# A fused gated linear attention and MLP kernel: the attention tiles of two neighbouring blocks follow each other

## The chip, the cores and the metric

The kernel runs on one core of a Trainium2 chip. Its time is device time in microseconds (us), and less is better. The engines work side by side, each through its own instructions in order: TensorE (PE in the profile; its weight loads are PEld) multiplies matrices into PSUM, VectorE (DVE), ScalarE (ACT) and GpSimd (POOL) do the rest, and SyncE (SP) issues the DMAs.

## The reference

The first part is a recurrence with a decay per key channel, for 4 batches, 8 heads, 768 steps and head size 48; the second is an MLP on its rows, 3072 x 384, with 2048 hidden units.

```
# attention: q, k, v, alpha are (4, 8, 768, 48)
for t in range(S):
    state = alpha[:, :, t, :, None] * state + einsum('bhd,bhe->bhde', k[:, :, t], v[:, :, t])
    y[:, :, t] = einsum('bhd,bhde->bhe', q[:, :, t], state)
x = y.transpose(0, 2, 1, 3).reshape(B * S, H * D)
# MLP: w_in (384, 2048), w_out (2048, 384), s and b one number each
r = maximum(x @ w_in, 0)
out = (s * r * r + b) @ w_out
```

## The kernel before

The 3072 rows are cut into 24 blocks of 128 steps, six per batch; the state is carried from block to block within a batch. For block n the work has these parts, each a small function:

- `load` (SP): four DMAs of 192 KB, for alpha, k, q and v, into rings of eight buffers. Blocks 0 to 3 are loaded two at a time (`load_pair`), and w_in and w_out in four pieces each.
- `ln` (ScalarE) takes the logarithm of alpha. `cum_pe` sums it over the steps with a triangular matrix `U_bf` on TensorE, and `cum_act` makes two exponentials of the sum. `decay`, inside `cum_act`, sends the last row through DRAM to the layout that the state needs (SP).
- `kb_mul`, `qb_mul` (VectorE) multiply k and q by these. `vcast` (GpSimd) brings v to bf16.
- `tr` (TensorE) transposes both into the bank `ct_ps`, and `qk_copy` brings them to SBUF as `qkT`.
- `amat` (TensorE, L343) makes the matrix A of one block: eight matmuls, over 48 rows each. Even heads use rows 0 to 47 of the array and write `a_ps[0]`, odd heads use rows 64 to 111 and write `a_ps[1]`. `mask` (VectorE, L352), once for each bank, multiplies A with a triangle (`mask4`) and writes bf16.
- `y_pe` (TensorE, L448 and L457) multiplies q by the carried state, and the masked A by v, into `y_ps`; `pst_pe` (L470) makes the block's own contribution to the state in `p_ps`. `y_act` (ScalarE) copies y. `t1` (VectorE) adds the state, and `sd` (GpSimd) decays it, into `sd_sb` for the next block and `sc_sb`.
- `xt_pe`, `xt_act` transpose y for the MLP (TensorE, ScalarE).
- `mp(n, u)` (TensorE, L555), for four quarters u of the hidden units: twelve matmuls. `rl` (ScalarE) is the ReLU, `sq` (VectorE) the square.
- `o_pe(n, u)` (TensorE, L586): four matmuls for each quarter, accumulated in `o_ps`. `o_out` copies the result, and later `add_bias` and `store` finish the first 14 blocks, since the bias row comes late: `colsum`, `bias_sum` and three `bias_row(i)` (TensorE, then ScalarE) make it. `bias_row` uses columns 384 to 511 of `y_ps`, `p_ps` and `y_ps` again.

The order is written out by hand. A list gives each call a position: in the list for the first blocks each entry stands 0.05 behind the last; behind position 60 they follow from formulas by block, with 8 units for a block. All events are sorted by position and issued in that order, so each engine works through its own part of it in order. Blocks 0 to 3 have pair forms of their own (`cum_pair`, `amat_pair`, `mask_pair`, `half_copy`, `y_pair`, `pst_pair`), and `busy` puts fill-in matmuls into the start. `mask_pair_sel` is a form of `mask_pair` that uses ScalarE and GpSimd in place of VectorE. `rooms` says which PSUM bank each early step uses; later the hidden units and the transposes of y take turns in the two `h_ps` banks.

Nothing in the program waits by time: an engine waits where data or a bank aren't ready.

Of the kernel before, what the change touches and what calls it, by code (L numbers as in the profile page):

```python
# [14 lines left out]
def kernel(  # L15
# [26 lines left out]
    NLD = 8  # L42
    PAIRS = [0, 2]
# [172 lines left out]
    def triangles():  # L216
        make_upper_triangular(nc, U_bf, 1.0, diag=True)
        for i in range(NP):
            make_upper_triangular(nc, mask4[:, i], 1.0, diag=True)
# [21 lines left out]
    def vcast(n):  # L241
        nc.gpsimd.tensor_copy(out=v_bf[n % 4], in_=raw("v", n))  # L242
# [94 lines left out]

    def amat(n):
        qkT = qkT_sb[n % 2]
        for p in range(NP):  # L340
            for e in range(2):
                r0 = 64 * e
                nc.tensor.matmul(  # L343
                    out=a_ps[e][:, p, :],
                    lhsT=qkT[r0 : r0 + 48, 1, p, :],
                    rhs=qkT[r0 : r0 + 48, 0, p, :],
                    start=True,
                    stop=True,
                )

    def mask(n, e):
        nc.vector.tensor_tensor(out=am_sb[e][n % 2], in0=a_ps[e], in1=mask4, op=ALU.mult)  # L352
# [125 lines left out]
    def y_act(n):  # L478
# [5 lines left out]
        ("A", 0, 0, 0): h0, ("A", 0, 0, 1): a0, ("A", 0, 1, 0): o, ("A", 0, 1, 1): a1, ("A", 2, 0, 0): ct,  # L484
        ("A", 2, 0, 1): o, ("A", 2, 1, 0): o, ("A", 2, 1, 1): ct, ("P", 1): h1, ("P", 3): h1, ("T", 0, 0): a1,
        ("T", 0, 1): ct, ("T", 1, 0): a0, ("T", 1, 1): o, ("T", 2, 0): h0, ("T", 2, 1): h0, ("T", 3, 0): o,
        ("T", 3, 1): ct, ("T", 4): a0, ("T", 5): a0, ("Y", 1): a0, ("Y", 3): a1, ("c", 0): h0, ("c", 1): o,
        ("c", 2): a0, ("c", 3): ct, ("c", 4): a1, ("o", 0): h0, ("o", 1): h1, ("o", 2): a1, ("o", 3): h1,
        ("t", 0): h0, ("t", 2): h0, ("x", 0): a1, ("x", 1): a0, ("x", 2): ct, ("x", 3): h1, ("x", 4): a0,
        ("x", 5): a0, ("x", 6): h0, ("x", 7): a0, (0, 0): a0, (0, 1): h0, (0, 2): ct, (0, 3): h0, (1, 0): o,  # L490
        (1, 1): o, (1, 2): h0, (1, 3): a0, (2, 0): ct, (2, 1): h0, (2, 2): a1, (2, 3): a1, (3, 0): ct, (3, 1): o,
        (3, 2): h1, (3, 3): h1, (4, 0): ct, (4, 1): o, (4, 2): ct, (4, 3): a0, (5, 0): a1, (5, 1): a0, (5, 2): h1,
        (5, 3): o, (6, 0): h0, (6, 1): o, (6, 2): h1, (6, 3): h1, (7, 0): h0, (7, 1): h1,
# [150 lines left out]
    load_pair(0, "v")  # L644
    load_pair(0, "k")
    load_pair(0, "q")
    load_pair(2, "al")
    load_pair(2, "q")
    load_pair(2, "k")
    load_one(4, al_sb, alpha)  # L650
    load_pair(2, "v")
    load_w_in(0)
    load_w_in(3)
# [3 lines left out]
    load_one(4, k_sb, k)  # L657
    load_one(5, al_sb, alpha)
    load_one(4, v_sb, v)
    load_w_out(0, 4)  # L660
    load_w_out(4, 8)
    load_w_out(8, 12)
    load_w_out(12, 16)
    load_one(6, al_sb, alpha)
    load_one(5, k_sb, k)
    load_one(5, q_sb, q)
    load_one(6, q_sb, q)
    load_one(6, k_sb, k)
    load_one(5, v_sb, v)
    load_one(7, v_sb, v)  # L670
    load_one(7, al_sb, alpha)
    load_one(6, v_sb, v)
    load_one(7, k_sb, k)
    load_one(7, q_sb, q)
# [38 lines left out]
    for pos, what in enumerate(  # L713
        [
            (ln, 0), (ln, 1), (busy, 1, ("c", 0)), (cum_pair, 0), (vcast, 1), (cum_act, 0), (spread,), (cum_pair, 1),
            (tot_pair, 0), (vcast, 0), (triangles,), (cum_act, 1), (kb_mul, 0), (busy, 1, ("T", 0, 1)), (tr, 0, 1),
            (kb_mul, 1), (pst_pair, 0), (half_copy, 0, 1, True), (tot_act, 0), (t1, 0, True), (qb_mul, 1),
            (busy, 1, ("T", 1, 0)), (tr, 1, 0), (ln, 2), (pst_pe, 5), (t1, 5), (qb_mul, 0), (sd, 5), (sd, 0), (tr, 0, 0),
            (half_copy, 1, 0), (ln, 3), (half_copy, 0, 0), (tr, 1, 1), (half_copy, 1, 1), (amat_pair, 0, 0),
            (mask_pair, 0, 0, 1), (mask_pair_sel, 0, 0, 0), (vcast, 3), (amat_pair, 0, 1), (cum_pair, 3),  # L720
            (mask_pair, 0, 1, 1), (mask_pair, 0, 1, 0), (vcast, 2), (cum_act, 3), (kb_mul, 3), (qb_mul, 3),
            (cum_pair, 2), (cum_act, 2), (tot_pair, 2), (ln, 4), (qb_mul, 2), (busy, 1, ("y", 0)), (y_pair, 0),
            (y_state, 1), (tot_act, 2), (tr, 3, 0), (t1, 1), (sd, 1), (tr, 3, 1), (y_act, 0), (y_act, 1),
            (half_copy, 3, 0), (tr, 2, 0), (half_copy, 3, 1, True), (half_copy, 2, 0), (busy, 1, ("x", 0)), (xt_pe, 0),
            (xt_pe, 1), (kb_mul, 2), (xt_act, 1), (xt_act, 0), (busy, 1, ("A", 2, 1, 0)), (amat_pair, 2, 1),
            (mask_pair_sel, 2, 1, 0), (tr, 2, 1), (cast_w_in, 0, 2, "act"), (cast_w_in, 0, 0, "act"),
            (mask_pair, 2, 1, 1), (pst_pair, 2), (half_copy, 2, 1), (t1, 2), (sd, 2), (amat_pair, 2, 0), (cum_pe, 4),
            (cum_act, 4), (cast_w_in, 0, 1, "dve"), (busy, 1, (0, 0)), (mp, 0, 0), (mask_pair, 2, 0, 1), (mp, 1, 0),
            (rl, 0, 0), (mask_pair, 2, 0, 0), (cast_w_in, 3, 2, "dve"), (cast_w_in, 3, 1, "dve"), (y_pair, 2),
            (y_state, 3), (cast_w_in, 3, 0, "act"), (mp, 0, 3), (rl, 1, 0), (y_act, 2), (xt_pe, 2), (mp, 1, 3), (t1, 3),  # L730
            (sq, 1, 0), (cast_w_in, 1, 0, "dve"), (sq, 0, 0), (cast_w_in, 1, 1, "dve"), (y_act, 3), (xt_act, 2),
            (rl, 0, 3), (cast_w_in, 1, 2, "dve"), (xt_pe, 3), (sq, 0, 3), (mp, 2, 0), (rl, 1, 3), (xt_act, 3),
            (mp, 2, 3), (sq, 1, 3), (cast_w_in, 2, 2, "dve"), (cast_w_in, 2, 0, "dve"), (cast_w_in, 2, 1, "dve"),
            (rl, 2, 0), (sq, 2, 0), (mp, 2, 1), (rl, 2, 1), (qb_mul, 4), (rl, 2, 3), (mp, 3, 0), (vcast, 4), (rl, 3, 0),
            (mp, 1, 1), (mp, 1, 2), (mp, 2, 2), (rl, 1, 1), (rl, 1, 2), (ln, 5), (rl, 2, 2), (tr, 4, 0), (sq, 2, 3),
            (kb_mul, 4), (tr, 4, 1), (sq, 1, 1), (sd, 3), (sq, 1, 2), (qk_copy, 4), (sq, 2, 1), (mp, 3, 3), (mp, 0, 2),
            (amat, 4), (rl, 3, 3), (rl, 0, 2), (mp, 3, 2), (mask, 4, 1), (mask, 4, 0), (sq, 2, 2), (mp, 3, 1),
            (cum_pe, 5), (y_pe, 4), (pst_pe, 4), (mp, 0, 1), (cast_w_out, 0, 2, False), (rl, 3, 2), (rl, 3, 1),
            (cast_w_out, 2, 4, False), (sq, 3, 3), (sq, 3, 0), (sq, 0, 2), (y_act, 4), (xt_pe, 4), (o_pe, 1, 0),
            (o_pe, 2, 0), (cum_act, 5), (cast_w_out, 6, 8, False), (colsum, 1), (t1, 4), (cast_w_out, 4, 6, False),  # L740
            (xt_act, 4), (mp, 4, 0), (cast_w_out, 8, 10, False), (rl, 4, 0), (rl, 0, 1), (mp, 4, 3), (mp, 4, 1),
            (mp, 4, 2), (o_pe, 1, 1), (rl, 4, 3), (cast_w_out, 10, 12, True), (o_pe, 1, 2), (rl, 4, 2), (sq, 4, 0),
            (sq, 4, 2), (cast_w_out, 12, 14, False), (ln, 6), (vcast, 5), (rl, 4, 1), (sd, 4), (o_pe, 2, 1),
            (cast_w_out, 14, 16, False), (kb_mul, 5), (sq, 4, 1), (sq, 0, 1), (sq, 3, 1), (o_pe, 0, 0), (qb_mul, 5),
            (o_pe, 2, 2), (cum_pe, 6), (load, 8), (o_pe, 1, 3), (o_pe, 2, 3), (o_out, 1), (o_pe, 4, 0), (o_out, 2),
            (o_pe, 4, 1), (tr, 5, 0), (tr, 5, 1), (cum_act, 6), (qb_mul, 6), (qk_copy, 5, True), (o_pe, 3, 0),
            (o_pe, 0, 1), (kb_mul, 6), (vcast, 7), (vcast, 6), (tr, 6, 0), (tr, 6, 1), (amat, 5), (qk_copy, 6, True),
            (ln, 7), (mask, 5, 1), (mask, 5, 0), (sq, 3, 2), (sq, 4, 3), (o_pe, 0, 2), (o_pe, 4, 2), (o_pe, 3, 1),
            (amat, 6), (cum_pe, 7), (mask, 6, 0), (mask, 6, 1), (cum_act, 7), (load, 9), (o_pe, 3, 2), (y_pe, 5),
            (y_act, 5), (pst_pe, 6), (o_pe, 0, 3), (xt_pe, 5), (qb_mul, 7), (kb_mul, 7), (t1, 6), (y_pe, 6),  # L750
            (o_pe, 4, 3), (tr, 7, 0), (load, 10), (load, 11), (tr, 7, 1), (o_out, 0), (o_pe, 3, 3), (xt_act, 5),
            (y_act, 6), (o_out, 4), (mp, 5, 3), (qk_copy, 7), (ln, 8), (colsum, 2), (amat, 7), (mask, 7, 1),
# [22 lines left out]
    def late(pos, *what):  # L775
        for fn, *args in what:
            if pos >= OPEN:
                at(pos, fn, *args)

    for n in range(4, NBLK):  # L780
        p = 8 * n
        f = max(0.0, min((n - 5) / 3.0, 1.0))
# [10 lines left out]
        if n + 4 < NBLK:  # L793
            late(p - 2.5, (load, n + NLD - 4))
# [38 lines left out]
```

## Time and profile before

| | us |
|---|---|
| median of three runs | 188.03 (187.07 to 189.16) |
| the profiled execution | 186.89 |
| its span, first to last instruction | 185.2 |
| TensorE busy | 178.8 (97%) |
| VectorE busy | 150.1 (81%) |
| ScalarE busy | 120.8 (65%) |
| GpSimd busy | 67.2 (36%) |

Busy time is the time in which an instruction of the engine is recorded. Matmuls overlap, since the next starts before the last has left the array, so for TensorE the distance from start to start says what a step costs. In a timeline line stand the start, the time covered, the engine, the line of the code, the operation, what it writes and reads, the shapes and the number of instructions taken together. The TensorE clock was granted in full during the whole span.

### The profile page before, as it was taken

To read this page: it belongs to the slowest core of one execution; us is meant where nothing else is said; L and a number is where in the kernel's file an instruction comes from. 1 tells how busy PE (TensorE), PEld (TensorE's weight loads), DVE (VectorE), ACT (ScalarE), POOL (GpSimd) and SP (SyncE) were. 2 spreads that over 40 slices of the span, in tenths; PEclk is the share of its full clock that TensorE was granted. 3 is DMA by queue.
4 is the path that set the end of the run, shared out by engine and by line. 5 is a ranking of instruction groups with operands and counts; after the bars stand their busy time and mean duration, and the time that the engine had idled before them with its cause. 6 is when DMAs were issued, how large, how long until landed. Compare 5 with 4: busy or idle time off the path is not lost.

```text
span 185.2 us, 6261 instructions
## 1 busy us (share of the span) xinstructions
PE 178.8 (97%) x2513; PEld 143.4 (77%) x2513; DVE 150.1 (81%) x304; ACT 120.8 (65%) x250; POOL 67.2 (36%) x110
## 2 busy tenths in 40 slices
PE   7978999999999999999999999999999999999993
PEld 2556899866688788788788788797787887888783
DVE  7589988984786779889779969699979999997641
ACT  3787988757596755775775777667566566564550
POOL 7989506004103244534006236155005275152000
PEclk9999999999999999999999999999999999999999
DMA  5999989969946980857685486597586785433213
GB/s 154 324 300 324 353 183 371 325 134 185 184 79 129 210 174 5 165 91 154 114 166 106 73 170 109 107 203 188 107 195 116 186 168 129 140 103 112 77 54 85
DMA packets 105262, 30.33 MB, mean 164 GB/s; under 512 B 98435, under 2 KB 103698, under 8 KB 105234
## 3 DMA queue, kind: packets, MB, share of 16 engines
q1 hardware_dynamic: 105230, 29.94, 69.6%
q8 instruction: 19, 0.31, 0.7%
q14 instruction: 9, 0.07, 0.1%
q10 hardware_dynamic: 4, 0.00, 0.0%
HBM read 25.19 MB, written 4.74 MB: 162 GB/s over the span
## 4 chain that ended last, share of the span: by engine, by line
PE 87%; SPq 5%; DMA 4%; ACT 1%; DVE 1%; issue 0%; ACTq 0%
PE h_ps L555 28%; PE o_ps L586 27%; PE ct_ps L315 4%; PE h_ps L586 4%; SPq L151 4%; DMA w_in_st<-in_moe_w_in_dram 4%; PE a_ps L343 3%; PE a_ps L555 3%; PE o_ps L555 2%; PE y_ps L457 2%; PE ct_ps L555 2%; PE h_ps L509 2%; PE ct_ps L247 2%; PE p_ps L470 1%; PE y_ps L448 1%; PE a_ps L612 1%
## 5 line engine op out<-in xcount | busy, mean ns | idle before, releaser
L555 PEld LDWEIGHTS <-w_in_bf 128*128 128x128 bf16 x1152 | 68.5, 98 | 6.0 <-ACT w_in_bf L173 0.7
L568 ACT ACTIVATE r_sb<-h_ps 128x512 bf16<-128x512 f32 x78 | 46.3, 597 | 31.7 <-PE h_ps L555 29.4
L555 PE MATMUL h_ps<-xd_all,w_in_bf 128*128 128x128 bf16 x936 | 62.5, 219 | 0.0
L586 PE MATMUL o_ps<-w_out_bf,gt_all 128*128 128x384 bf16 x304 | 61.2, 326 | 0.1
L575 DVE TENSOR_TENSOR gt_all<-r_sb 128x512 bf16<-128x512 bf16 x96 | 45.2, 484 | 19.3 <-ACT r_sb L568 18.6
L541 POOL TENSOR_TENSOR sd_sb<-t_sb,blast 48x192 bf16<-48x192 f32 x40 | 20.9, 523 | 73.4 <-DVE t_sb L531 37.8
L586 PEld LDWEIGHTS <-gt_all 128*128 128x128 bf16 x368 | 32.7, 98 | 16.8
L242 POOL CAST v_bf<-v_sb 128x384 bf16<-128x384 f32 x24 | 17.4, 733 | 26.5 <-DMA v_sb<-in_v_dram 17.4
L545 POOL TENSOR_TENSOR sc_sb<-t_sb,blast 112x384 f32<-112x384 f32 x16 | 19.6, 1227 | 1.3
L307 DVE TENSOR_TENSOR qb_sb<-q_sb,b_sb 128x384 bf16<-128x384 f32 x24 | 16.0, 672 | 1.8 <-ACT b_sb L261 1.2
L352 DVE TENSOR_TENSOR am_b<-a_ps,mask 128x512 bf16<-128x512 f32 x20 | 13.6, 682 | 3.4 <-PE a_ps L343 3.3
L516 ACT ACTIVATE xd_all<-h_ps 128x384 bf16<-128x384 bf16 x18 | 8.8, 491 | 10.4 <-PE h_ps L509 10.4
L234 ACT ACTIVATE la_sb<-al_sb 128x384 bf16<-128x384 f32 x24 | 12.3, 519 | 3.9 <-DVE blast L702 2.2
L304 DVE TENSOR_TENSOR kb_sb<-k_sb,bi_sb 128x384 bf16<-128x384 f32 x24 | 13.6, 570 | 1.5 <-DMA k_sb<-in_k_dram 0.8
L352 DVE TENSOR_TENSOR am_a<-a_ps,mask 128x512 bf16<-128x512 f32 x20 | 13.6, 681 | 0.4 <-PE a_ps L343 0.4
L327 DVE COPY qkT<-ct_ps 112x1024 bf16<-112x1024 bf16 x17 | 11.6, 681 | 1.5 <-PE ct_ps L315 1.5
L479 ACT ACTIVATE y_bf<-y_ps 128x384 bf16<-128x384 f32 x22 | 10.8, 490 | 0.9 <-PE y_ps L457 0.6
L260 ACT ACTIVATE bi_sb<-ct_ps 128x384 f32<-128x384 f32 x20 | 9.7, 487 | 1.7 <-PE ct_ps L247 1.6
L315 PEld LDWEIGHTS <-qb_sb 128*112 128x112 bf16 x96 | 8.2, 130 | 2.6 <-DVE qb_sb L307 1.2
L261 ACT ACTIVATE b_sb<-ct_ps 128x384 f32<-128x384 f32 x20 | 9.9, 497 | 0.0
L586 PE MATMUL h_ps<-w_out_bf,gt_all 128*128 128x384 bf16 x48 | 9.4, 326 | 0.0
L637 DVE TENSOR_TENSOR w_in_st<-w_in_st,bias_w 128x384 f32<-128x384 f32 x14 | 8.6, 613 | 0.0
(150 smaller groups left out, 248.0 us busy)
## 6 DMA issues: line engine op xcount, KB each, us to landing
al_sb<-in_alpha_dram SPq DMA_DIRECT2D x20, 192.0 KB
q_sb<-in_q_dram SPq DMA_DIRECT2D x20, 192.0 KB
k_sb<-in_k_dram SPq DMA_DIRECT2D x20, 192.0 KB
v_sb<-in_v_dram SPq DMA_DIRECT2D x20, 192.0 KB
w_in_st<-in_moe_w_in_dram SPq DMA_DIRECT2D x4, 768.0 KB
w_out_st<-in_moe_w_out_dram SPq DMA_DIRECT2D x4, 768.0 KB
out_dram<-w_in_st SPq DMA_DIRECT2D x10, 192.0 KB
out_dram<-out_sb SPq DMA_DIRECT2D x5, 192.0 KB
```

Of the source, the lines that this page charges most:

```text
L234: nc.scalar.activation(out=la_sb[n % 2][:, :, 0:48], in_=raw("al", n), func=AF.Ln)
L242: nc.gpsimd.tensor_copy(out=v_bf[n % 4], in_=raw("v", n))
L304: nc.vector.tensor_tensor(out=kb_sb[n % 4][:, :, 0:48], in0=raw("k", n), in1=bi_sb[n % 2], op=ALU.mult)
L307: nc.vector.tensor_tensor(out=qb_sb[n % 2][:, :, 0:48], in0=raw("q", n), in1=b_sb[n % 3], op=ALU.mult)
L315: nc.tensor.transpose(out=t_bank(n, x if n in pair_of else None)[0:112, x, p, :], in_=t.rearrange("a h d -> a (h d)")[:, 128 * p : 128 * p ...
L352: nc.vector.tensor_tensor(out=am_sb[e][n % 2], in0=a_ps[e], in1=mask4, op=ALU.mult)
L541: nc.gpsimd.tensor_tensor(out=sd[r, :, d], in0=t1_sb[r, :, d], in1=bl[r].to_broadcast([48, NP, 48]), op=ALU.mult)
L545: nc.gpsimd.tensor_tensor(out=sc_sb[0:112], in0=t1_sb[0:112], in1=bl[0:112].to_broadcast([112, NP, 96]), op=ALU.mult)
L555: nc.tensor.matmul(out=hp[:, jj * C : (jj + 1) * C], lhsT=w_in_bf[:, kk, 128 * j : 128 * (j + 1)], rhs=xd_sb[n][:, kk], start=(kk == 0), s ...
L568: nc.scalar.activation(out=rs, in_=room((g, u)), func=AF.Relu)
L575: nc.vector.tensor_tensor(out=gt_sb[g][:, u * 512 : (u + 1) * 512], in0=rs, in1=rs, op=ALU.mult)
L586: nc.tensor.matmul(out=op[:, 0:d_model], lhsT=gt_sb[n][:, j * C : (j + 1) * C], rhs=w_out_bf[:, j, :], start=(j == 0), stop=(j == NJ - 1),)
```

## The change

From block 10 on the A tiles of an even block and the odd one after it follow each other on TensorE. The odd block's A tiles go to `y_ps` and `p_ps` in place of `a_ps`. The positions of nearly all steps of a block from there on come from a table, one row for even and one for odd blocks. The list for the first blocks, the order of the early loads and the banks of the early steps are new as well; `mask4` is filled from `U_bf` by one copy in place of four triangles made on GpSimd, and `vcast` has a form for ScalarE.

```diff
+    ADJ = 10
...
-    def triangles():
+    def triangle():
         make_upper_triangular(nc, U_bf, 1.0, diag=True)
-        for i in range(NP):
-            make_upper_triangular(nc, mask4[:, i], 1.0, diag=True)
+
+    def triangles(act=False):
+        rows = U_bf.rearrange("a (o t) -> a o t", o=1).to_broadcast([128, NP, 128])
+        if act:
+            nc.scalar.activation(out=mask4, in_=rows, func=AF.Copy)
+        else:
+            nc.vector.tensor_copy(out=mask4, in_=rows)
...
-    def vcast(n):
-        nc.gpsimd.tensor_copy(out=v_bf[n % 4], in_=raw("v", n))
+    def vcast(n, act=False):
+        if act:
+            nc.scalar.activation(out=v_bf[n % 4], in_=raw("v", n), func=AF.Copy)
+        else:
+            nc.gpsimd.tensor_copy(out=v_bf[n % 4], in_=raw("v", n))
...
+    def a_bank(n):
+        if n >= ADJ and n % 2:
+            return [b.rearrange("a (p t) -> a p t", p=NP) for b in (y_ps, p_ps)]
+        return a_ps
...
-                    out=a_ps[e][:, p, :],
+                    out=a_bank(n)[e][:, p, :],
...
-        nc.vector.tensor_tensor(out=am_sb[e][n % 2], in0=a_ps[e], in1=mask4, op=ALU.mult)
+        nc.vector.tensor_tensor(out=am_sb[e][n % 2], in0=a_bank(n)[e], in1=mask4, op=ALU.mult)
...
     load_pair(0, "al")
-    load_pair(0, "v")
     load_pair(0, "k")
     load_pair(0, "q")
+    load_pair(0, "v")
     load_pair(2, "al")
+    load_one(4, al_sb, alpha)
+    load_pair(2, "k")
     load_pair(2, "q")
-    load_pair(2, "k")
-    load_one(4, al_sb, alpha)
     load_pair(2, "v")
     load_w_in(0)
-    load_w_in(3)
     load_w_in(1)
     load_w_in(2)
     load_one(4, q_sb, q)
     load_one(4, k_sb, k)
+    load_one(4, v_sb, v)
+    load_w_in(3)
+    load_w_out(4, 8)
+    load_w_out(0, 4)
+    load_w_out(12, 16)
+    load_w_out(8, 12)
+    load_one(5, k_sb, k)
     load_one(5, al_sb, alpha)
-    load_one(4, v_sb, v)
-    load_w_out(0, 4)
...
+    places = [
+        {"ln": -19.57, "vcast": -16.5, "cum": -16.47, "qk": -16.4, "tr": -11.12, "cp": -10.71, "A": -5.83, "ma": -5.6,
+         "y": -0.98, "st": 0.18, "load": -9.48, "xt": 2.48, "m": (6.34, 7.54, 6.34, 7.79), "o": (8.05, 9.65, 10.72, 15.01)},
+        {"ln": -23.72, "vcast": -27.33, "cum": -17.24, "qk": -17.05, "tr": -15.26, "cp": -14.29, "A": -13.65, "ma": -13.36,
+         "y": -0.1, "st": 0.95, "load": -6.75, "xt": 1.89, "m": (4.54, 6.24, 7.73, 8.38), "o": (8.61, 11.63, 13.7, 14.36)},
+    ]
...
+        w = {"ln": -c - 1.9, "vcast": 0.01 - c, "cum": -c, "qk": 0.2 - c, "tr": -t, "cp": 0.001 - t, "A": -a,
+             "ma": 0.001 - a, "y": 0.0, "st": 0.0, "load": -2.5, "xt": 1.0, "m": (2.5, 3.5, 5.5, 7.5),
+             "o": (8.5, 9.5, 12.5, 14.5)}
+        if n >= ADJ:
+            w = places[n % 2]
```

Each `late(p + w[...], ...)` then takes its position from `w`. Of the new list for the first blocks these lines matter most; the first is the beginning, the rest leads to the first MLP matmuls:

```diff
+            (ln, 0), (triangle,), (ln, 1), (busy, 1, ("c", 0)), (cum_pair, 0), (cum_act, 0), (kb_mul, 0), (qb_mul, 0),
...
+            (tr, 2, 1), (mask_pair, 2, 1, 1), (mask_pair, 2, 1, 0), (xt_act, 1), (cast_w_in, 0, 0, "dve"),
+            (cast_w_in, 0, 2, "dve"), (sd, 1), (cum_pe, 4), (half_copy, 2, 1, True), (amat_pair, 2, 0), (pst_pair, 2),
+            (mask_pair, 2, 0, 0), (t1, 2), (sd, 2), (mask_pair, 2, 0, 1), (cast_w_in, 0, 1, "act"), (mp, 0, 0),
+            (mp, 1, 0), (cum_act, 4), (rl, 0, 0), (cast_w_in, 1, 1, "dve"), (vcast, 4), (cast_w_in, 1, 2, "act"),
+            (cast_w_in, 1, 0, "act"), (sq, 0, 0), (y_pair, 2), (t1, 3), (y_state, 3), (mp, 0, 1), (y_act, 2), (xt_pe, 2),
```

## The prediction

> **What bounds the kernel now.** I read the page's busy table and slices first, then the chain that ended last in order of time, then the TensorE timeline of one block, then VectorE.
>
> ```profile
> span 185.2 us, 6261 instructions
> PE 178.8 (97%) x2513; PEld 143.4 (77%) x2513; DVE 150.1 (81%) x304; ACT 120.8 (65%) x250; POOL 67.2 (36%) x110
> ...
> PE   7978999999999999999999999999999999999993
> ```
>
> TensorE is busy in nearly every slice. Its ends are modelled, so the chain has to say whether it waits:
>
> ```profile
> 10.16 7.60 DMA w_in_st<-in_moe_w_in_dram
> 17.78 1.16 ACT w_in_bf L173 x2
> 18.99 0.84 PE a_ps L555 x12
> ...
> 73.42 0.67 PE h_ps L555 x12
> ...
> 80.01 0.45 PE ct_ps L315 x8
> 80.46 0.67 PE h_ps L555 x12
> ```
>
> Two stretches are to be seen. Until 18.99 us TensorE has no MLP matmuls, because the first quarter of w_in lands at 17.78 us and two casts on ScalarE follow. From there to the end the chain runs on TensorE almost alone: twelve mp matmuls every 0.67 us (0.056 each), four o_pe matmuls every 0.65, and one block from 73.42 to 80.46, 7.04 us. So time can come only from an earlier 18.99, from fewer or cheaper TensorE steps, or it is lost to new waits on TensorE. This is one block's middle, on TensorE:
>
> ```profile
> 80.96 0.81 PE L586 MATMUL o_ps<-w_out_bf,gt_all 128*128 128x384 bf16 x4
> 81.61 0.83 PE L555 MATMUL h_ps<-xd_all,w_in_bf 128*128 128x128 bf16 x12
> 82.28 0.34 PE L448 MATMUL y_ps<-sd_sb,qkT 112*128 112x96 bf16 x4
> 82.45 0.19 PE L457 MATMUL y_ps<-v_bf,am_a 128*128 128x48 bf16 x1
> ...
> 82.66 0.33 PE L470 MATMUL p_ps<-v_bf,kb_sb 128*128 128x96 bf16 x4
> 82.92 0.40 PE L343 MATMUL a_ps<-qkT 48*128 48x128 bf16 x8
> 83.25 0.82 PE L586 MATMUL o_ps<-w_out_bf,gt_all 128*128 128x384 bf16 x4
> 83.92 0.33 PE L509 MATMUL h_ps<-ident,y_bf 128*128 128x128 bf16 x3
> ```
>
> The A matmuls (L343) use 48 rows, two at a time in the two halves of the array, and around them time is lost. Entering: four matmuls of 96 columns take 82.45 - 82.28 = 0.17 us at L448, but from L470 to L343 it is 82.92 - 82.66 = 0.26; 0.09 lost. Inside: four concurrent pairs at 0.056 would be 0.22, but 83.25 - 82.92 = 0.33; 0.11 lost. After: the next four o_pe matmuls take 83.92 - 83.25 = 0.67 instead of 0.65; 0.02. Together **0.22 us for each time that TensorE goes into the half-array form and out again**.
>
> **The change, part by part.** The sum is made against the profiled execution: 186.89 us, a span of 185.2 and 1.69 around it. It lies 0.6% under the median of the runs shown, 188.03; I carry the difference over as a ratio.
>
> *A tiles in pairs.* From block 10 to 23 amat(n) for even n stands at 8n - 5.83, and for the odd block at 8(n+1) - 13.65 = 8n - 5.65, with no TensorE event between. Seven pairs, each with one entry and exit fewer: 7 x 0.22 = **-1.54 us**. No TensorE work is added; A needs the same eight matmuls. The Trainium skill, "TensorEngine Tiling (Array Packing)", section "Key Properties", says that a change of tiling mode drains the engine; "TensorE: Matmul & The Clock Gate", section "Single matmul latency", puts a matmul whose drain isn't hidden at (398 + N)/2.4 ns. That would be 0.16 us above the 0.056 spacing at each of two switches, so 7 x 0.33 = 2.3 us, and the sum would end 0.8 lower; the rows above show two thirds of it, and they decide.
>
> *The odd block's banks.* Its A tiles go to y_ps and p_ps, whole banks, 512 columns. The next y_pe and pst_pe of the even block come four steps later (o_pe, two mp, o_pe: 2.64 us), and four masks have to be read out first. For the price I need two VectorE rows:
>
> ```profile
> 52.76 0.40 PE L343 MATMUL a_ps<-qkT 48*128 48x128 bf16 x8
> ...
> 53.20 0.69 DVE L352 TENSOR_TENSOR am_b<-a_ps,mask 128x512 bf16<-128x512 f32 x1
> ...
> 53.81 0.68 DVE L352 TENSOR_TENSOR am_a<-a_ps,mask 128x512 bf16<-128x512 f32 x1
> ```
>
> A mask starts 0.04 after the A group's end (53.16) and masks follow every 0.60. Counted from the even block's first A matmul: masks start at 0.44, 1.04, 1.64 and 2.24 and the last ends at 2.92. TensorE leaves the pair at 0.46 + 0.11 = 0.57, and y_pe starts at 0.57 + 2.64 = 3.21, pst_pe 0.38 later. Both are free: no cost.
>
> But bias_row(0) and bias_row(2) also write y_ps, columns 384 to 511, which the odd block's third mask reads. They stand at 108.6 and 124.6, just after mp(13,0) at 108.54 and mp(15,0) at 124.54, so TensorE reaches them at 0.57 + 0.65 + 0.67 = 1.89 after the pair's start. The third mask ends at 1.64 + 0.68 = 2.32, and with 0.04 until TensorE starts that is 2.36: a **new wait of 0.47 us, twice, +0.94**. Behind it on TensorE stand mp(13,1), o_pe(12,3), y_pe(14); nothing makes it up, as TensorE has no idle time. Before, bias_row met a y_ps free for two microseconds. It is 0 if the masks were done by then, and 0.47 + 0.60 each if VectorE is one mask late. I take 0.47: every mask row shows 676 to 693 ns.
>
> *The odd block's qk_copy.* Before, tr stood 2.9 positions (2.5 us, at 7.04 us for 8) before amat. Now the odd block has between them o_pe (0.65), xt_pe (0.17), the entry (0.09) and the even A (0.22): 1.13 us. The copy needs 0.16 (rest of the last transpose) + 0.04 + 0.68 + 0.04 = 0.92. It fits by 0.21 if VectorE is free. Ahead of it on VectorE stand kb_mul, qb_mul, two sq, t1, and for n >= 14 o_out: by their rows (0.47, 0.47, 0.34, 0.34, 0.47, 0.47 from start to start) they finish about 0.2 before the transposes do. So I take 0, with up to +0.6 in a pair as the other end.
>
> *The start.* The same TensorE work as before precedes mp(0,0). The first casts go to VectorE twice (0.34 apart) and ScalarE once (0.62), so mp(0,0) could start at 17.78 + 0.34 + 0.42 = 18.54 instead of 18.99. But y_pair(2) now waits for mask_pair(2,0,1), which stands on VectorE behind those casts, mask_pair(2,0,0) and t1(2): 17.78 + 0.67 + 0.60 + 0.47 + 0.68 = 20.20, against 20.34 before. mp(0,1) also wants two ScalarE casts of w_in's second quarter, behind relu(0,0): about 21.1 against mp(0,3) at 21.29 before. So **-0.2**, between -0.45 (all of the first step) and +0.5 (VectorE late with its extra masks; one mask_pair moved there from ScalarE and POOL). Four triangles fewer on POOL and three fill-in matmuls fewer (0.22 each) lie before 18.99 in waiting time: 0. vcast(1) goes from POOL to ScalarE in the same waiting time, qk_copy(5) to VectorE (0.68) and qk_copy(8) to ScalarE (1.02 in the rows of blocks 5 and 6), with over 1.3 us of o_pe behind each; the copy that fills mask4 stands ahead of mask(4,1) with slack: 0.
>
> *Loads.* w_in's last quarter now lands behind three block tiles, about 27 us, and mp(1,3) is the thirteenth mp instead of the tenth, about 29.5. w_out lands about as it is used, and o_pe starts three mp later. No cost, up to +1.0 if the casts queue. On SP the loads come earlier than before relative to ln, and decay's copies stay 14 us ahead of sd: 0.
>
> *A stall that goes.* The chain has a piece at 131.87 to 132.86, where add_bias holds up VectorE and TensorE loses 0.2; its place is another now: **-0.2**.
>
> Sum: 186.89 - 1.54 + 0.94 - 0.2 - 0.2 = **185.9**, that is 0.995 of the profiled execution, and 187.0 on the median.
>
> **The rivals.**
>
> *Only the gain is real.* If the two bias waits are hidden and the start keeps its 0.45, the sum is 186.89 - 1.54 - 0.45 - 0.2 = 184.7, 185.8 on the median, 1.2% faster. For it: VectorE idles before these masks in the rows above. Against: three masks at 0.60 are longer than TensorE's 1.89.
>
> *VectorE comes too late for the odd A (slower).* Place: qk_copy of the odd block. Price: what its cover lacks, in each pair. For it is this row:
>
> ```profile
> L307 DVE TENSOR_TENSOR qb_sb<-q_sb,b_sb x24: 544/553/1183, 7.9 to 163.3; 128x384 bf16<-128x384 f32 x24
> ```
>
> qb_mul takes 1.18 instead of 0.55 when POOL's sc_sb runs beside it, +0.63. With one such product ahead of the copy in every pair the cover lacks 0.63 - 0.21 - 0.2 = 0.22: the saved drain is eaten up, 7 x 0.22 = 1.54 on top of 185.9, 187.4, or 188.6 on the median. With an add_bias (0.47) there as well it lacks 0.69: 185.9 + 4.8 = 190.7, 191.9 on the median. It decides from 0.14 us of lateness per pair (1.0 / 7), and from 0.41 (2.9 / 7) the kernel is over 1% slower. Against: sd follows t1, and behind t1 VectorE now reads PSUM five times (the copy, four masks), forms that no row shows slowed. [...]
>
> *The new start stalls TensorE.* Everything up to block 9 is reordered, and the old order lost under 1 us after 18.99. Casts of the late w_in quarter and of w_out, or the load of block 8 issued about 5 us later than before, would each hold TensorE for 0.5 to 1.5: 186.9 to 188, 188 to 189 on the median.
>
> **How the numbers follow.** The forecast (a gain under 1%) has 0.54; only the gain, 0.22; late VectorE, 0.12; a stalling start, 0.12, half of it over 1%. One per cent, 1.9 us, is about what a measurement of this kernel can tell from no change. Faster: 0.22 and a little of the forecast, 0.25. Slower: most of late VectorE and half of the start, 0.17. The forecast's own range is 186.0 to 188.0; the range down to the first rival less the runs' scatter (185.3) and up into the slower cases (189.5).
>
> **What would show it.** Sixteen A matmuls in a row with one gap before and one after; two blocks from tr to tr in 13.86 us instead of 14.08; bias_row for y_ps starting right after a mask's end, 0.4 late; mp(0,0) near 18.5; no TensorE wait on qk_copy. It is wrong if the odd A matmuls wait for VectorE, if TensorE waits between 19 and 60 us, or if the drain saved isn't near 0.22.

## The result, and the profile after

The changed kernel is slower by half a per cent: 188.56 us (median of 22 executions, 187.58 to 192.08) against 187.83 us for the kernel before on the same chip (22 executions, 186.33 to 189.17), a ratio of 1.0049 with a 95% interval of 1.0025 to 1.0073. The ratios, here and below, leave out executions that ran slow as a whole (192.08 and 191.70 here), so they are not the quotients of the medians. That is within the one per cent that the prediction counted as no change, but on the other side of it. The profiled execution has a span of 187.6 us; the page begins so:

```profile
span 187.6 us, 6221 instructions
PE 179.5 (96%) x2510; PEld 143.3 (76%) x2510; DVE 144.4 (77%) x301; ACT 123.1 (66%) x255; POOL 59.0 (31%) x97
...
PE   7988999999999999799899999999999999999993
```

Two dips are new in TensorE's slices (a 7 and an 8, near 76 and 91 us). First, what was meant to happen: the A tiles of blocks 12 and 13 in TensorE's timeline.

```profile
94.20 0.33 PE L523 MATMUL h_ps<-ident,y_bf 128*128 128x128 bf16 x3
94.46 0.40 PE L357 MATMUL a_ps<-qkT 48*128 48x128 bf16 x8
94.69 0.22 PE L357 MATMUL y_ps<-qkT 48*128 48x128 bf16 x1
...
94.86 0.22 PE L357 MATMUL p_ps<-qkT 48*128 48x128 bf16 x1
95.01 0.82 PE L600 MATMUL o_ps<-w_out_bf,gt_all 128*128 128x384 bf16 x4
```

The even block's eight matmuls start at 94.46, the odd block's 0.23 later with no loss between (four concurrent pairs at 0.056 are 0.22), and o_pe follows 0.32 after that. One entry and one exit, as foreseen. Then the waits of TensorE (line, waited for, total, times, longest):

```profile
PE y_ps L462 <- POOL sd_sb L555: 1.8, 2, 1.1
...
PE y_ps L210 <- DVE am_a L366: 0.3, 1, 0.3
```

The kernel before had no wait of y_pe on `sd_sb`. The two are here in TensorE's timeline:

```profile
75.33 0.83 PE L569 MATMUL h_ps<-xd_all,w_in_bf 128*128 128x128 bf16 x12
77.25 0.33 PE L462 MATMUL y_ps<-sd_sb,qkT 112*128 112x96 bf16 x4 [1.09 <-POOL sd_sb L555]
...
92.08 0.33 PE L462 MATMUL y_ps<-sd_sb,qkT 112*128 112x96 bf16 x4 [0.75 <-POOL sd_sb L555]
```

These are y_pe(9) and y_pe(11). From start to start, less what the matmuls between cost, TensorE loses 1.25 and 0.91 us there. GpSimd's timeline says why (in brackets: its idle time before, and what ended it):

```profile
72.20 0.96 POOL L251 CAST v_bf<-v_sb 128x384 bf16<-128x384 f32 x2 [5.28 <-DMA v_sb<-in_v_dram]
75.48 1.72 POOL L555 TENSOR_TENSOR sd_sb<-t_sb,blast 48x192 bf16<-48x192 f32 x2 [2.32 <-DMA blast<-row_dr]
...
89.31 1.48 POOL L251 CAST v_bf<-v_sb 128x384 bf16<-128x384 f32 x2 [8.19 <-PE h_ps L569]
90.75 1.28 POOL L555 TENSOR_TENSOR sd_sb<-t_sb,blast 48x192 bf16<-48x192 f32 x2
```

and in the kernel before:

```profile
71.80 1.39 POOL L541 TENSOR_TENSOR sd_sb<-t_sb,blast 48x192 bf16<-48x192 f32 x2 [4.20 <-DVE kb_sb L304]
...
84.21 1.08 POOL L541 TENSOR_TENSOR sd_sb<-t_sb,blast 48x192 bf16<-48x192 f32 x2 [3.66 <-DVE t_sb L531]
85.35 0.80 POOL L242 CAST v_bf<-v_sb 128x384 bf16<-128x384 f32 x1
```

sd(8) waits for decay's copy `blast`. In the SP queue its first half, row(8), is issued at 69.56 instead of 67.29. SP's queue before:

```profile
67.29 0.61 SPq L296 DMA_DIRECT2D row_dr<-b_sb  x1
69.90 0.82 SPq L298 DMA_DIRECT2D blast<-row_dr  x2
```

and after:

```profile
66.46 0.75 SPq L132 DMA_DIRECT2D k_sb<-in_k_dram  x1
67.25 0.68 SPq L132 DMA_DIRECT2D q_sb<-in_q_dram  x1
67.98 1.48 SPq L132 DMA_DIRECT2D v_sb<-in_v_dram  x1
69.56 0.38 SPq L305 DMA_DIRECT2D row_dr<-b_sb  x1
72.08 0.82 SPq L307 DMA_DIRECT2D blast<-row_dr  x2
```

And sd(10), which ran at 84.21 before, ahead of the next casts, now runs at 90.75 behind two of them: vcast(13), moved to 27.33 positions ahead of its block, and vcast(12). Not all of the difference is their work: t1(10), which sd(10) needs, now ends at 87.60. The trace names a TensorE instruction as what vcast(13) waited for, but its v was issued by SP at 85.56, about 4 us ahead, and in the profiles further down the same wait is put down to that DMA.

The last is bias_row, on VectorE and then on TensorE:

```profile
124.86 0.68 DVE L366 TENSOR_TENSOR am_a<-y_ps,mask 128x512 bf16<-128x512 f32 x1
...
125.59 0.49 PE L210 MATMUL y_ps<-cs_sb,ones_f 128*128 128x128 f32 x2 [0.33 <-DVE am_a L366]
```

The third mask ends at 125.54 and bias_row(2) starts at 125.59. Against the TensorE work between, the loss is 0.49 us, and 0.26 at bias_row(0).

### The profile page after: what moved, and what is told of

The parts are those of the page before. It is cut to its first block, busy times and chain, and to the rows that moved or that the text cites. A ratio compares the mean times of both kernels' runs of the same rounds, so it can differ in the third digit from the quotient of the medians.

```text
span 187.6 us, 6221 instructions
## 1 busy us (share of the span) xinstructions
PE 179.5 (96%) x2510; PEld 143.3 (76%) x2510; DVE 144.4 (77%) x301; ACT 123.1 (66%) x255; POOL 59.0 (31%) x97
## 4 chain that ended last, share of the span: by engine, by line
PE 80%; DVE 6%; DMA 5%; POOL 2%; ACT 2%; issue 2%; SPq 1%; DVEq 0%; POOLq 0%; ACTq 0%
PE o_ps L600 24%; PE h_ps L569 24%; PE ct_ps L324 4%; PE h_ps L600 3%; PE o_ps L230 2%; PE a_ps L357 2%; PE a_ps L569 2%; POOL sd_sb L555 2%; DMA al_sb<-in_alpha_dram 2%; PE y_ps L471 2%; PE ct_ps L569 2%; DMA blast<-row_dr 2%; PE y_ps L462 2%; PE h_ps L523 2%; PE o_ps L569 1%
## 5 line engine op out<-in xcount | busy, mean ns | idle before, releaser
L600 PE MATMUL o_ps<-w_out_bf,gt_all 128*128 128x384 bf16 x320 | 64.0, 326 | 0.0
L569 PE MATMUL h_ps<-xd_all,w_in_bf 128*128 128x128 bf16 x948 | 60.6, 219 | 0.0
L589 DVE TENSOR_TENSOR gt_all<-r_sb 128x512 bf16<-128x512 bf16 x96 | 41.9, 455 | 17.5 <-ACT r_sb L582 17.3
L555 POOL TENSOR_TENSOR sd_sb<-t_sb,blast 48x192 bf16<-48x192 f32 x40 | 26.9, 673 | 49.4 <-DVE t_sb L545 32.4
L251 POOL CAST v_bf<-v_sb 128x384 bf16<-128x384 f32 x23 | 13.6, 614 | 62.6 <-DMA v_sb<-in_v_dram 51.3
L316 DVE TENSOR_TENSOR qb_sb<-q_sb,b_sb 128x384 bf16<-128x384 f32 x24 | 14.2, 594 | 2.3 <-ACT b_sb L270 1.4
L559 POOL TENSOR_TENSOR sc_sb<-t_sb,blast 112x384 f32<-112x384 f32 x16 | 13.8, 860 | 1.3
L240 ACT ACTIVATE la_sb<-al_sb 128x384 bf16<-128x384 f32 x24 | 12.5, 530 | 2.3 <-DVE blast L716 2.3
L366 DVE TENSOR_TENSOR am_a<-a_ps,mask 128x512 bf16<-128x512 f32 x13 | 8.9, 687 | 3.7 <-PE a_ps L357 3.5
L366 DVE TENSOR_TENSOR am_b<-a_ps,mask 128x512 bf16<-128x512 f32 x13 | 8.9, 682 | 1.7 <-PE a_ps L357 1.7
L324 PEld LDWEIGHTS <-kb_sb 128*112 128x112 bf16 x96 | 7.2, 130 | 0.8 <-DVE kb_sb L313 0.4
```

What stands on the lines that cost most here:

```text
L240: nc.scalar.activation(out=la_sb[n % 2][:, :, 0:48], in_=raw("al", n), func=AF.Ln)
L316: nc.vector.tensor_tensor(out=qb_sb[n % 2][:, :, 0:48], in0=raw("q", n), in1=b_sb[n % 3], op=ALU.mult)
L324: nc.tensor.transpose(out=t_bank(n, x if n in pair_of else None)[0:112, x, p, :], in_=t.rearrange("a h d -> a (h d)")[:, 128 * p : 128 * p ...
L366: nc.vector.tensor_tensor(out=am_sb[e][n % 2], in0=a_bank(n)[e], in1=mask4, op=ALU.mult)
L555: nc.gpsimd.tensor_tensor(out=sd[r, :, d], in0=t1_sb[r, :, d], in1=bl[r].to_broadcast([48, NP, 48]), op=ALU.mult)
L559: nc.gpsimd.tensor_tensor(out=sc_sb[0:112], in0=t1_sb[0:112], in1=bl[0:112].to_broadcast([112, NP, 96]), op=ALU.mult)
```

## The experiments

Ratios are to the kernel before, measured on the same chip beside it. "Loss" is TensorE's distance from start to start less what the matmul costs there without a wait.

### Which half of the change costs: the start alone, the rest alone

`new_start` keeps everything new up to block 9 and takes the old formulas from block 10 on:

```diff
-    ADJ = 10
+    ADJ = 99
```

> The new start and load order, with the old formulas from block 10 on (no neighbouring A tiles, no odd-block banks). Theory (the new start's order on SyncE makes sd(8) late): y_pe(9) waits about 1.2 us for sd(8) here too, and with the start's other waits the kernel takes 1.3 to 1.8 us more than before (ratio 1.007 to 1.010). Rival (the loss comes from the new positions from block 10 on): no wait of over 0.3 us at y_pe(9), and the time of before within 0.5 us.

Measured: 187.02 us, ratio 0.9971 (0.9945 to 0.9997). The new start by itself is a little faster. `new_rest` is the other half: the old start, loads and triangles, with the new positions and banks from block 10:

```diff
+    ADJ = 10
...
+    def a_bank(n):
...
+    places = [
...
+        if n >= ADJ:
+            w = places[n % 2]
```

> The start of before, with the new positions, the neighbouring A tiles and the odd block's banks from block 10 on. Theory: 1.5 us saved by seven tiling changes fewer, 0.75 lost to the two bias rows, 0.4 to qk_copy; y_pe(9) does not wait; the wait of 0.9 us at y_pe(11) stays or shrinks, since GpSimd's order is the same but loads are issued 2 us earlier. Together 0.5 to 1.0 us less than before with the last wait gone, about equal with it. Rival (the new positions are what costs): over 0.5 us more than before.

Measured: 187.86 us, ratio 1.0021 (0.9991 to 1.0051). Its profile has the losses at y_pe(11), 0.91, and at the two bias_row, 0.38 and 0.49; `new_start` has none of them. So these three belong to the positions from block 10. The wait at y_pe(9) is in neither, though `new_start` has the new order on SP and issues row(8) at 69.29. My theory that the SP order alone makes that wait fell.

### The wait at y_pe(9): load(8) back ahead of decay

`load8` puts the loads of block 8 back to where they are issued before the decay copies of blocks 6 and 7:

```diff
-            (sq, 4, 0), (cum_pe, 5), (cum_act, 5), (o_pe, 2, 2), (o_pe, 0, 2), (o_pe, 2, 3), (ln, 6), (cum_pe, 6),
+            (sq, 4, 0), (cum_pe, 5), (cum_act, 5), (o_pe, 2, 2), (o_pe, 0, 2), (o_pe, 2, 3), (ln, 6), (cum_pe, 6), (load, 8),
...
-            (tr, 7, 0), (tr, 7, 1), (vcast, 7), (xt_pe, 6), (load, 8), (t1, 6), (load, 9), (load, 10), (qk_copy, 7),
+            (tr, 7, 0), (tr, 7, 1), (vcast, 7), (xt_pe, 6), (t1, 6), (load, 9), (load, 10), (qk_copy, 7),
```

> The changed kernel with the load of block 8 put back ahead of the decay copies of blocks 6 and 7 on SyncE, nothing else. Theory (these copies, each of which makes SyncE wait some 2.3 us, delay 16 bulk loads and so the decay copy of block 8): row 8 is issued about 2 us earlier, the wait of 1.25 us at y_pe(9) falls under 0.2, 1.0 to 1.3 us less than the changed kernel. Rival (GpSimd's vcast(11), which stands ahead of sd(8) and waits for its data, is what makes sd(8) late): the wait at y_pe(9) stays above 0.8.

Measured: 188.44 us, ratio 1.0040 (1.0005 to 1.0075). row(8) is issued at 67.00 and sd(8) runs at 71.47; no wait at y_pe(9). But the 1.0 to 1.3 us expected did not come: the time hardly moves, so that wait is not what makes the median.

`again` is the changed kernel once more, for how often it comes.

> The changed kernel once more, to see which of its waits stand in every execution. Theory: the wait at y_pe(11) (0.9 us, GpSimd's order) and the two at the bias rows (0.4 and 0.5) come back within 0.1; the one at y_pe(9) hangs on when one small copy lands, with about 1 us of margin, and lies anywhere from 0 to 1.3. Rival (SyncE's late order makes it in every execution): 1.0 us or more again.

Measured: 188.28 us, ratio 1.0052 (1.0020 to 1.0085): the result repeats. GpSimd's timeline in this execution:

```profile
72.84 1.15 POOL L556 TENSOR_TENSOR sd_sb<-t_sb,blast 48x192 bf16<-48x192 f32 x2 [0.46 <-DMA blast<-row_dr]
...
87.70 2.08 POOL L252 CAST v_bf<-v_sb 128x384 bf16<-128x384 f32 x2 [7.49 <-DMA v_sb<-in_v_dram]
89.75 1.28 POOL L556 TENSOR_TENSOR sd_sb<-t_sb,blast 48x192 bf16<-48x192 f32 x2
```

Same program, but sd(8) ran at 72.84, not 75.48, and y_pe(9) does not wait. With the new order on SP and the new positions sd(8) ends 2.0 to 2.3 us ahead of y_pe(9) in four profiles; with the old order on SP it is 2.8 to 3.2 in `load8`, `new_rest`, `both_bias` and `clear`, but 2.05 in `apart` and in the kernel before. So the SP order costs about one of three microseconds at most, and no wait follows from that alone: in the first profile the second `blast` copy of 0.8 KB went out at 72.45 and sd(8) started 3.0 us later, here at 71.31 and 1.5 us later. That copy landed late by itself; why is not shown. The loss at y_pe(11) is 0.91 here as well.

### The wait at y_pe(11): the cast ahead of sd(10)

`vcast` brings the odd block's cast back to where the kernel before has it, behind sd of the blocks two and three before:

```diff
-        {"ln": -23.72, "vcast": -27.33, "cum": -17.24, "qk": -17.05, "tr": -15.26, "cp": -14.29, "A": -13.65, "ma": -13.36,
+        {"ln": -23.72, "vcast": -14.8, "cum": -17.24, "qk": -17.05, "tr": -15.26, "cp": -14.29, "A": -13.65, "ma": -13.36,
```

> The changed kernel with vcast of odd blocks from 10 on put back to 14.8 positions ahead of its block in place of 27.33, behind sd of the even block, nothing else. Theory (vcast(13), which waits for its data, holds up sd(10) on GpSimd): the wait of 0.91 us at y_pe(11) goes, and the one at y_pe(9) stays at 1.0 to 1.3, for that one comes from SyncE; about 0.9 us less than the changed kernel. Rival (both waits come from GpSimd's order): both go, 2.1 us less. Rival (both come from SyncE): both stay.

Measured: 186.97 us, ratio 0.9989 (0.9963 to 1.0015), some 0.6% or 1.1 us less than the whole change. GpSimd:

```profile
87.61 2.45 POOL L555 TENSOR_TENSOR sd_sb<-t_sb,blast 48x192 bf16<-48x192 f32 x2 [5.57 <-DVE t_sb L545]
90.13 0.58 POOL L251 CAST v_bf<-v_sb 128x384 bf16<-128x384 f32 x1
```

sd(10) starts when t1(10) is done, and TensorE's y_pe(11), at 91.10, waits for nothing. vcast(12) still stands ahead of sd(10), but it is done at 82.04: it is vcast(13), with its late v, that must not stand there. So the cast's position makes the wait. Its size was still odd: 0.91 in five profiles, though the cast for block 13 started anywhere from 86.75 to 89.31. It lasted 2.06 us in `load8`, 2.05 in `new_rest`, 1.44 in `again` and 0.83 in the first profile, and each time ended 0.36 after VectorE's first square behind `colsum`. The second half of sd(10) in `vcast` does the same: it takes 1.88 of the 2.45 us above and ends at 90.06, 0.36 after that square, in time for y_pe(11). So I tried what VectorE does there. `col5` moves one column sum out of that stretch:

```diff
-        at(69.3 + 8 * (i - 3), colsum, i)
+        at(88.6 if i == 5 else 69.3 + 8 * (i - 3), colsum, i)
```

> The changed kernel with one edit: the column sum of block step 5 (VectorE, 0.95 us) is issued behind kb_mul and qb_mul of block 13 instead of ahead of the two squares before them. The order on GpSimd stays: casts of v for blocks 13 and 12, then sd(10). Theory A, GpSimd is held: in four executions the cast for block 13 started at 86.75 to 89.31 us and lasted 2.06 to 0.83 us, and each time ended 0.36 after the end of the square that follows the column sum without a gap; so its end, and with it the 0.91 us that TensorE waits for sd(10) at y_pe(11), hangs on that unbroken stretch of VectorE. Without the column sum in it the stretch ends 0.87 earlier: the wait falls to between 0 and 0.4 (the more the later v of block 13 lands) and the median by about 0.5 to 0.9. Theory B, only the late data of block 13 holds GpSimd: the wait stays at 0.9 and the cast lasts as long as before. Either way the two waits of bias_row stay at 0.38 and 0.49.

Measured: 187.18 us, ratio 0.9992 (0.9967 to 1.0016). VectorE of `again`, in the time of the casts shown above:

```profile
86.89 0.69 DVE L337 COPY qkT<-ct_ps 112x1024 bf16<-112x1024 bf16 x1 [0.28 <-PE ct_ps L325]
87.50 0.95 DVE L204 TENSOR_TENSOR cs_sb<-cs_sb,w_out_st 128x768 f32<-128x768 f32 x1
88.36 1.06 DVE L590 TENSOR_TENSOR gt_all<-r_sb 128x512 bf16<-128x512 bf16 x2
```

VectorE of `col5`:

```profile
86.55 0.69 DVE L336 COPY qkT<-ct_ps 112x1024 bf16<-112x1024 bf16 x1 [0.28 <-PE ct_ps L324]
87.91 1.40 DVE L589 TENSOR_TENSOR gt_all<-r_sb 128x512 bf16<-128x512 bf16 x2 [0.67 <-ACT r_sb L582]
```

GpSimd of `col5`:

```profile
86.96 0.95 POOL L251 CAST v_bf<-v_sb 128x384 bf16<-128x384 f32 x2 [7.08 <-DMA v_sb<-in_v_dram]
87.88 1.15 POOL L555 TENSOR_TENSOR sd_sb<-t_sb,blast 48x192 bf16<-48x192 f32 x2
```

Without the sum, both casts take 0.95 together instead of 2.08, and y_pe(11) loses nothing, although the order on GpSimd is the same. Theory A holds: two things make the wait, the casts ahead of sd(10), and VectorE's column sum and square, during which GpSimd's cast makes hardly any headway. The sum's new place costs 0.3 at one odd A, whose qk_copy it now delays. By the rows that leaves a gain of 0.6 us on the whole change; the ratios say 1.1, and they are not sharp enough to tell the two apart. The bias losses are 0.38 and 0.49 as before.

### The wait of bias_row

`bias` moves the calls to where no mask of an odd block reads `y_ps`:

```diff
-        at(108.6 + 8 * i, bias_row, i)
+        at((112.0, 116.6, 118.0)[i], bias_row, i)
```

> The changed kernel with the three bias_row calls at 112.0, 116.6 and 118.0 instead of 108.6, 116.6 and 124.6, where y_ps isn't read by a mask of an odd block. By the sum of the prediction the two waits of bias_row (0.38 and 0.49 in the profiles so far) go, and nothing else changes: y_pe(11) waits 0.91 as before, and the median is 0.9 us lower than the changed kernel's, a ratio near 1.000 to the kernel before. If the masks only move the wait to the next step on TensorE, the time stays at the changed kernel's 1.005.

Measured: 186.86 us, ratio 0.9989 (0.9958 to 1.0020). Both losses are gone, y_pe(11) still loses 0.91, and the ratio is 0.006, or 1.1 us, under the whole change's: the sum said 0.94, the rows 0.87.

### All three together, and the drain by itself

`both_bias` has the edits of `load8`, `vcast` and `bias`.

> The changed kernel with the load of block 8 ahead of the decay copies, vcast of odd blocks at 14.8 positions, and bias_row(0) and (2) at 112.0 and 118.0, where y_ps is free. Theory: no wait of TensorE over 0.2 us at y_pe(9), y_pe(11) and the bias rows; 0.9 + 0.86 less than the changed kernel's steady waits, so 0.3 to 0.9% less time than before (ratio 0.991 to 0.997). Rival (waits removed come back elsewhere, since VectorE or the loads then bound): ratio 0.999 or more.

Measured: 185.94 us, ratio 0.9884 (0.9836 to 0.9933), faster than both kernels; span 184.3. The ratio lies below the range expected, but it rests on four executions. After 24 us no loss above 0.27 is left. Its A tiles of blocks 12 and 13 and what follows them:

```profile
92.39 0.40 PE L357 MATMUL a_ps<-qkT 48*128 48x128 bf16 x8
92.62 0.22 PE L357 MATMUL y_ps<-qkT 48*128 48x128 bf16 x1
...
92.94 0.82 PE L600 MATMUL o_ps<-w_out_bf,gt_all 128*128 128x384 bf16 x4
```

`apart` is the same kernel with the odd block's A moved behind an o_pe, so that the A tiles are no longer neighbours:

```diff
-"tr": -15.26, "cp": -14.29, "A": -13.65, "ma": -13.36,
+"tr": -15.26, "cp": -14.29, "A": -12.9, "ma": -12.89,
```

> As both_bias, but amat and mask of odd blocks follow one o_pe step later (12.9 and 12.89 positions in place of 13.65 and 13.36), so that the A tiles of two blocks are no longer neighbours; banks and all other places stay. Theory (going into the half-array form and out costs 0.22 us): seven more entries and exits, 1.5 us more than both_bias less 0.15 to 0.4 of waits on qk_copy, which now has another 0.65 us; 1.1 to 1.5 us more in all. Rival (the drain is hidden by other work, or the neighbours wait as long as they save): within 0.4 us of both_bias.

```profile
93.21 0.40 PE L357 MATMUL a_ps<-qkT 48*128 48x128 bf16 x8
93.54 0.82 PE L600 MATMUL o_ps<-w_out_bf,gt_all 128*128 128x384 bf16 x4
94.30 0.23 PE L357 MATMUL y_ps<-qkT 48*128 48x128 bf16 x1
...
94.63 1.51 PE L569 MATMUL h_ps<-xd_all,w_in_bf 128*128 128x128 bf16 x24
```

Measured: 187.61 us, ratio 0.9996 (0.9970 to 1.0022). From `both_bias` that is 1.67 us by the medians, 2.1 by the ratios, more than the 1.1 to 1.5 expected; the intervals, 0.005 and 0.010 wide, can't settle the size. The lines can: four o_pe cost 0.65, so 94.30 - 93.54 - 0.65 = 0.11 on entering, and 94.63 - 94.30 - 0.22 = 0.11 inside and on leaving. All seven odd A show the same, 1.5 us together. The saving is real.

`clear` goes on from `both_bias` and takes the two VectorE steps away that stand ahead of an odd qk_copy: bias_sum at 107.0, add_bias and store of block 6 later by 2.4.

```diff
-    at(103.3, bias_sum)
+    at(107.0, bias_sum)
...
+        late_by = 2.4 if n == 6 else 0.0
+        at(125.3 + 4.55 * n + late_by, add_bias, n)
```

> As both_bias, but bias_sum and the seventh add_bias moved on VectorE behind the four masks, out of the way of qk_copy(15) and qk_copy(21). Theory (these two additions make the odd A matmuls wait): no gap over 0.06 us between the A matmuls of a pair; 0.14 to 0.4 us less than both_bias. Rival (another instruction is what makes qk_copy late): the gaps stay.

Measured: 185.88 us, ratio 0.9901 (0.9865 to 0.9937). All seven odd A start 0.23 to 0.24 after the even one, so the losses of 0.11 and 0.13 at two of them are gone, but against `both_bias` the time can't be told apart.

## Why the prediction was right or wrong

The prediction was 187.0 us, 0.995 of the kernel before; measured was 1.0049. The range holds it, but a gain was forecast and a loss came.

**The drain (into the half-array form and out), -1.54: right.** 0.22 was read from rows; `apart` against `both_bias` gives 0.22 in its lines and 0.24 by the medians. The estimate by the formula from the Trainium skill that the prediction set beside it ("TensorE: Matmul & The Clock Gate", section "Single matmul latency") is 0.33; the runs side with the rows.

**bias_row, +0.94: right,** mechanism and size: 0.38 and 0.49 in most profiles, and `bias` takes them out. What the first lacks is lost just before, at the odd A of that pair: 0.11 there, or 0.23 in the first profile, where bias_row then loses 0.26.

**The start, -0.2: not settled.** mp(0,0) started at 18.59 (foreseen 18.54), but between 17.69 and 19.98 in the other profiles with this start, and in several it then waits once more for a cast of w_in (0.84 us in `new_start`). y_pair(2) came as foreseen, at 20.17; y_state(3) behind it lost up to 0.33 waiting for sd(2), so mp(0,1) is at 21.45, not 21.1, and at 21.19 to 22.55 in the others, where the kernel before has mp(0,3) at 21.29. Only two of the ten profiles with the new start are ahead of before at this point. Yet `new_start` as a whole gained 0.3% (0.0 to 0.55).

**The odd qk_copy, 0: nearly.** Five of seven pairs lose nothing, two 0.11 to 0.23, where bias_sum or add_bias stands ahead. That is the place of the rival "VectorE comes too late", but two pairs and not seven. The stall of add_bias at 132 us did go: TensorE's losses from 132 us on fall from 1.89 to 0.97, which is that stall (0.19), three drains (0.64) and two small losses at 169.6 and 174.0 us (0.22), less 0.13 for an odd A.

**The step that failed is "Loads": "On SP the loads come earlier than before relative to ln, and decay's copies stay 14 us ahead of sd: 0", and what it leaves out, GpSimd.** The table of places moves vcast of an odd block n ahead by 12.5 positions, past sd(n-2) and sd(n-3). I followed the moved steps on TensorE, VectorE, ScalarE and SP, and priced only vcast(1), in the start. On GpSimd vcast(13) and vcast(12) now stand ahead of sd(10), VectorE's column sum holds them, and TensorE waits 0.91 in every profile that has this position and the column sum beside it. On SP the claim is false too: the loads of block 8 now come behind the decay copies of blocks 6 and 7, and row(8) went out 2.3 us later. The 14 us were not there even before: the `blast` copies of block 8 were issued at 69.90, 1.9 us ahead of sd(8). sd(8) ends some 2 us ahead of y_pe(9); once, with a late copy, that was too little, and 1.25 was lost.

With +0.91 in it, the prediction's sum is 185.9 + 0.9 = 186.8, or 1.000; two small new losses before xt_pe(8) and a tr near 77 us (0.27 and 0.16) make it 187.2, or 1.002. The remaining 0.003 is not settled. The spread of the start is a candidate, but `new_start` measured faster than before. The wait at y_pe(9) is another, but `load8` without it measured 1.0040, and the halves (0.9971 and 1.0021) multiply to 0.9992; the intervals are 0.005 to 0.007 wide.

## What to carry to other kernels

When an order is rewritten, go through every engine's own queue, the idle ones too, and ask of each moved instruction whose data it waits for and who stands behind it: here GpSimd, busy 31%, took back 0.91 of the 1.54 us saved on TensorE by one cast placed too early. Where a moved step shares a bank or a queue with a rare one (three bias rows, one column sum), mend the rare one: here three small moves turned 0.5% slower into 1% faster.

## What the runs showed of the hardware that was not expected

- A GpSimd cast of 128x384 took 0.50 us alone and up to 2.06 beside VectorE's column sum and square, two tensor_tensor instructions with both inputs in SBUF, back to back; VectorE's sum took its usual 0.95. The cast ended 0.36 after the square, however early it had begun. Beside VectorE's qk_copy, which reads PSUM, it took 0.50 (`col5`). The Trainium skill, "SBUF — State Buffer", section "Who interferes with whom", says that a VectorE instruction with two inputs in SBUF contends with a GpSimd instruction that reads SBUF; these rows agree. That whoever issues first keeps the ports for the whole instruction it says of the modes in which VectorE takes both, which tensor_tensor does not have; here the cast had been issued first (86.75 against 87.16 in `load8`) and was the one held.
- The same `blast` copy of 0.8 KB, in two executions of the same program: sd(8), which waited for it, started 3.0 us after its issue in one (72.45 to 75.48) and 1.5 us in the other (71.31 to 72.84).
